# A recurrent-attention and token/channel-mixer kernel: batch 0's attention laid out by token slot, other filler matmuls, and a new instruction order

## The chip, the core and the metric

The kernel runs on one core of a Trainium2 chip. The core has a matrix engine (TensorE, PE in the profile; its weight loads are PEld), a vector engine (VectorE, DVE), an activation engine (ScalarE, ACT), a general engine (GpSimd, POOL) and a sync engine (SyncE, SP) that here only issues transfers. Each engine works through its own queue in program order; semaphores order work between engines. Matrix results land in PSUM, eight banks of 128 partitions by 512 float32; everything else lives in SBUF. The metric is the device time of one execution in microseconds, the median of several runs.

## The reference

```python
for t in range(S):                                   # attention: B, H, S, D = 4, 8, 768, 48
    state = alpha[:, :, t, :, None] * state + einsum('bhd,bhe->bhde', k[:, :, t], v[:, :, t])
    y[:, :, t] = einsum('bhd,bhde->bhe', q[:, :, t], state)
x = y.transpose(0, 2, 1, 3).reshape(4, 768, 384)
h = relu(x.transpose(0, 2, 1) @ w_tok1) @ w_tok2     # tokens: 768 -> 256 -> 768
u = x + h.transpose(0, 2, 1)
out = u + relu(u @ w_ch1) @ w_ch2                    # channels: 384 -> 1536 -> 384
```

Inputs and output are float32. Each of q, k, v and alpha is 4.7 MB, the weights are 6.3 MB and the output is 4.7 MB.

## The kernel before, in words

**Attention.** Each batch is cut into three tiles of 256 tokens; tile n (0 to 11) belongs to batch n // 3. A tile's tokens lie two to a partition: partition p holds tokens 2p (slot 0) and 2p+1 (slot 1). A chunk is 128 tokens, partitions 0 to 63 or 64 to 127, so a tile has two chunks (hf 0 and 1). For a tile the names in the program are: `ld_at`, `ld_kt`, `ld_qt`, `ld_vt` (loads of 393 KB each); `ln` or `ln1`/`lnP` (logarithm of alpha); `cum` or `cumw` (running sums of the logarithms by matmuls with a triangular matrix); `E` and `IE` (exp of the sums and of their negatives, on ACT); `kk` and `qq` (k times IE, q times E, in bf16); `vb` (v in bf16); `trk`, `trq` (PE transposes of kk and qq) and `evk`, `evq` (their copies out of PSUM); `G` (products of keys and queries per head, one per chunk), `mask` (causal mask, on DVE, also the copy out of PSUM); `K` (k times v, summed over a chunk), `s`, `sa`, `sm` (the recurrent state after a chunk); `ia`, `ib` (query times state), `y` (masked G times v, added to it in PSUM) and `x` (copy out, the mixer's input).

Tiles 0 to 2 are "wide": both slots go through `lnw`, `cumw`, `E`, `IE`. In tiles 3 to 11 slot 0's decay is folded in by products instead (`P`, `r1`, `k0a`, `q0r`). From tile 6 on the transposes are made by DMA (`dk`, `dq`, then `pq`).

In the kernel before, `G` by chunk puts slot 0's tokens of a chunk on partitions 0 to 63 and slot 1's on 64 to 127, so `y` can contract 128 tokens in one matmul of 128 rows. For that v has to be moved across partitions (`vs0`, `vs1`: `vswap`), and so have the keys for `K` (`ka`, `kb`, `kc`: `kturn`): copies of 64 partitions by 384 on ACT or POOL. `K` (`kfull`) is then four 128-row matmuls of 96 columns per chunk. The state is carried by `sa` (K plus old state, on DVE) and `sm` (times the decay, on DVE or POOL).

**Mixer.** For each batch: `t1` (12 matmuls of 384 columns, w_tok1), `ht` (relu), `t2` (12 matmuls, w_tok2), `u` (add, DVE), then u transposed: for batches 0 and 1 by PE (`up`, and `ut` copies it out), for 2 and 3 by DMA (`ux`); `c1` (24 groups of three matmuls, w_ch1), `rt` (relu, 24 on ACT or DVE), `c2` (24 groups of three, w_ch2), `o` (add, DVE) and `st` (store). Weights come in 16 loads of 393 KB (`ldw_`) and are cast to bf16 (`cw_`).

**Order.** The program is written under a manual schedule: the text ORDER lists every operation in the order of issue with the letter of its engine (t PE, s ACT, v DVE, g POOL, y SP), and BUFS gives each value its buffer. Dependencies between operations become semaphore waits. One more rule is in `shared`: operations that two engines run over a common SBUF port (the products, casts and shifts on DVE and POOL, those with `port=True`) are made to wait for the last such operation of the other engine, so the two never run them at once.

**Fillers.** `f1_...` and `f3_...` in ORDER are one or three matmuls of 512 columns of zeros into a bank that the next operation overwrites; nobody reads them. They stand before work of tiles 0 to 2 only.

The opening of ORDER before, up to the last `t1` of batch 0's first half:

```
ld_at1s ld_at0y ld_qt0y ld_vt0y ld_kt0s ld_at2y f1_cumw0t ln0s f3_cumw0t f1_trk1t f1_cumw1t f1_trk0t f3_cumw1t
f1_trq0t f3_trq0t ln1s ld_qt1y f1_trq1t cumw0t cumw1t E0s ld_at3y f3_trk1t IE0s Et0s qq0v vb0s ld_kt1y kk0v trq0t E1s
...
ldw_wt10s sa0_1v f1_y0t lnP3s qq2v IE2s Et2s ldw_wt11y cum3t ib0t IE3s r13s sm0_1v trq2t E3s evq2s G0_1t y1_0t sa1_1v
vb3g vs1_3s x1_0s G1_1t kk3v f1_y2t ldw_wt21y ld_qt3y mask1_1v kk2g ldw_wt20y f1_y1t mask0_1v vb2s ib1t y1_1t trk3t
vs0_2g vs1_2g trk2t evk3v ia1t ldw_wc13y f3_G02t f1_G02t sm1_1g evk2v kc2s ld_at5y P4g cw_wt10s x1_1v K2t ldw_wc14y
G0_2t sa0_2v cw_wt11s mask0_2v sm0_2g ka3s ln14s t1_0_0_0t ia2t G1_2t y0_1t t1_0_1_0t t1_0_1_1t y0_2t t1_0_0_1t vs0_3g
mask1_2v kc3s x0_1s ib2t kb3s lnP4s t1_0_1_2t ldw_wc15y q0r3v x0_2s y1_2t K3t t1_0_0_2t t1_0_1_3t ld_kt4y x1_2s qq3v
```

Of the kernel before, what the change touches and what calls it, by code (L numbers as in the profile page):

```python
# [96 lines left out]
NB = 3  # L97
NX = 6
# [12 lines left out]
WIDE = (0, 1, 2)  # L111

# [3 lines left out]
def build(g):  # L116
# [8 lines left out]
    def filler(nm, bank):  # L125
        return [P.op(f"f{z}_{nm}", {"PE": pe([512] * z)["PE"], "NONE": (0.0, 0.0)}, -100, writes=[bank],
                     emit=lambda e, z=z: g.fill(bank, z)) for z in (1, 3)]

    def attention(n):
# [8 lines left out]
        def fill(nm, bank):  # L138
            return filler(f"{nm}{n}", bank) if n < NB else []

        at, kt, qt, vt = V("in"), V("in"), V("in"), V("in")
        ld = {}
        for v, nm in ((at, "at"), (kt, "kt"), (qt, "qt"), (vt, "vt")):
            ld[nm] = P.op(f"ld_{nm}{n}", {"SP": (420.0, 420.0), "ACT": (374.0, 374.0)}, -90000.0 + 10 * n, writes=[v],
                          emit=lambda e, v=v, nm=nm: g.load(e, nm, v, b, k, ld[nm]), dma=("i", IN_NS, 1500.0, 650.0))
        la, E, IE = V("la"), V("E"), V("IE")
        pkk, pkq, vb = V("pkk"), V("pkq"), V("vb")
        k_in, q_in = [ld["kt"]], [ld["qt"]]
        if n in WIDE:
            lnp = O("ln", act(800, True), 0, writes=[la], reads=[at], preds=[ld["at"]], emit=lambda e: g.lnw(la, at))  # L150
            cb = V("pair")
            cum = O("cumw", pe([384] * 4 + [4] * 8 + [16]), 2, writes=[cb, E, IE], reads=[la], preds=[lnp] + fill("cumw", cb),
                    emit=lambda e: g.cumw(cb, la))
            e1 = O("E", act(768), 4, writes=[E], reads=[cb], preds=[cum], emit=lambda e: g.exps(E, cb, 1.0))
            et = O("Et", act(16), 6, writes=[E], reads=[cb], preds=[cum], emit=lambda e: g.exptot(E, cb))
            e2 = O("IE", act(768), 3, writes=[IE], reads=[cb], preds=[cum], emit=lambda e: g.exps(IE, cb, -1.0))
        else:
# [8 lines left out]
            e1 = et = O("E", act(400), 4, writes=[E], reads=[cb], preds=[cum], emit=lambda e: g.expE(E, cb))  # L166
            e2 = O("IE", act(384), 4, writes=[IE], reads=[cb], preds=[cum], emit=lambda e: g.expIE(IE, cb))
# [12 lines left out]
        if n < NX:  # L180
            bk, bq = V("one"), V("one")
            trk = O("trk", pe([128] * 8), 8, writes=[bk], reads=[pkk], preds=[kk] + fill("trk", bk),
                    emit=lambda e: g.trw(bk, pkk))
            evk = O("evk", either(dve(1024, True), act(1024)), 9, writes=[tpk], reads=[bk], preds=[trk],
                    emit=lambda e: g.trwev(e, tpk, bk))
            trq = O("trq", pe([128] * 8), 8, writes=[bq], reads=[pkq], preds=[qq] + fill("trq", bq),
                    emit=lambda e: g.trw(bq, pkq))
            evq = O("evq", either(dve(1024 * 1.065), act(1024 * 1.34)), 9, writes=[tpq], reads=[bq], preds=[trq],
                    emit=lambda e: g.qev(e, tpq, g.bank(bq).bitcast(BF16)))
        else:  # L190
            evk = O("dk", {"SP": (1240.0, 1240.0)}, 9, writes=[tpk], reads=[pkk], preds=[kk],
                    emit=lambda e: g.xbar(tpk, pkk), dma=("x", 1400.0, 1180.0, 480.0))
# [13 lines left out]
        nst = 2 if k < NB - 1 else 1
        kp = V("pair")
# [149 lines left out]
    for b in range(B):  # L357
        mixer(b)
# [91 lines left out]
class Emit:  # L450


    def __init__(self, tc, ctx, q, k, v, alpha, w, out):
# [61 lines left out]
        for t in self.T["pkq"] + self.T["pkk"]:  # L515
            dv.memset(t[:, :, :, D:64], 0.0)
# [358 lines left out]
```

## Time and profile before

| what | value |
|---|---|
| time, median of 3 runs (lowest to highest) | 167.82 us (167.51 to 168.41) |
| span of the profiled execution (its own time, first to last instruction) | 165.0 us |
| PE busy | 156.2 us, 95% |
| DVE, ACT, POOL busy | 121.2, 96.2, 68.7 us |
| transfers | 34.48 MB, 209 GB/s over the span |
| instructions | 4235 |

The span counts from the first instruction to the last; the run's time has in addition what lies before and after them, 2.8 us between the profiled span and the median. "Busy" of PE counts a matmul until its results are out, so back-to-back matmuls overlap, and it counts the fillers as well; only the spacing of matmuls says how fast the engine takes them. A row of the timeline gives start, length, engine, line, operation, operands and count, and in brackets how long the engine was idle before it and what ended that. A row of the chain gives start, length and what was running; "SPq" is the transfer queue of SP.

### The profile page before, as it was taken

What the parts mean: (1) busy time and instruction counts of PE and PEld (TensorE: products, weight loads), DVE (VectorE), ACT (ScalarE), POOL (GpSimd) and SP (SyncE); (2) the same over time, 40 slices, a digit from 0 to 9 for tenths busy, and PEclk for the clock granted to TensorE, in tenths of its full rate; (3) what the DMA queues carried; (4) which work ended last, traced back from release to release, by engine and by line L of the source; (5) the groups of instructions that cost most, each with busy time, mean ns of one, the idle gap of its engine ahead of it and who ended that gap; (6) DMA issues with size and microseconds to landing.
All of it is one profiled execution on the core that took longest, in us unless ns stands there. A gap on an engine that the chain in (4) does not pass through costs nothing.

```text
span 165.0 us, 4235 instructions
## 1 busy us (share of the span) xinstructions
PE 156.2 (95%) x1683; PEld 99.2 (60%) x1683; DVE 121.2 (73%) x210; ACT 96.2 (58%) x186; POOL 68.7 (42%) x84
## 2 busy tenths in 40 slices
PE   7969769999999999999999999999999999999992
PEld 2435446666666766576666666666666656656662
DVE  4098989989898898798878999989492455524422
ACT  3599987998877837939887746913614001514110
POOL 4025659497217475792388528973300000000000
PEclk9999999999999999999999999999999999999999
DMA  4999999999999999999989996898001136200213
GB/s 121 324 325 325 337 347 316 365 327 352 371 335 347 326 315 226 307 252 264 136 198 255 211 250 120 219 181 183 0 4 48 49 75 157 105 0 0 99 72 119
DMA packets 74531, 34.48 MB, mean 209 GB/s; under 512 B 67984, under 2 KB 73488, under 8 KB 74512
## 3 DMA queue, kind: packets, MB, share of 16 engines
q1 hardware_dynamic: 50576, 23.30, 55.2%
q10 hardware_dynamic: 23936, 10.91, 24.3%
q8 instruction: 13, 0.21, 0.5%
q14 instruction: 6, 0.05, 0.1%
HBM read 25.17 MB, written 4.72 MB: 181 GB/s over the span
## 4 chain that ended last, share of the span: by engine, by line
PE 83%; DMA 4%; SPq 3%; POOL 2%; issue 2%; ACT 2%; DVE 1%; POOLq 0%; DVEq 0%
PE ps L816 29%; PE ps L811 29%; PE ps L593 14%; PE ps L792 5%; DMA in<-in_v_dram 4%; PE ps L787 4%; SPq L534 3%; PE ps L654 1%; PE ps L803 1%; POOL pkk L642 1%; DVE gtm L700 1%; POOL vb L685 1%; ACT x L684 1%; POOL ss L753 1%; ACT E L626 0%
## 5 line engine op out<-in xcount | busy, mean ns | idle before, releaser
L816 PE MATMUL ps<-wc,rt 128*128 128x384 bf16 (+1 forms) x300 | 54.7, 320 | 0.0
L811 PE MATMUL ps<-ut,wc 128*128 128x384 bf16 x288 | 51.3, 326 | 0.0
L782 ACT ACTIVATE rt<-ps 128x384 bf16<-128x384 f32 x54 | 24.4, 490 | 35.4 <-PE ps L811 34.7
L811 PEld LDWEIGHTS <-wc 128*128 128x128 bf16 x288 | 27.1, 98 | 16.7
L816 PEld LDWEIGHTS <-rt 128*128 128x128 bf16 x300 | 27.5, 98 | 15.9
L700 DVE TENSOR_TENSOR gtm<-ps,mk 128x1024 bf16<-128x1024 f32 x24 | 28.7, 1219 | 4.8 <-PE ps L593 3.4
L784 DVE TENSOR_SCALAR rt<-ps 128x384 bf16<-128x384 f32 x42 | 21.7, 551 | 9.2 <-PE ps L811 9.2
L820 DVE TENSOR_TENSOR o<-ps,u 128x384 f32<-128x384 f32 (+1 forms) x25 | 13.1, 537 | 10.0 <-PE ps L816 9.1
L685 POOL CAST vb<-in 64x384 bf16<-64x384 f32 (+1 forms) x18 | 10.9, 608 | 15.2 <-DVE pkk L642 8.9
L593 PE MATMUL ps<-zs 128*128 128x512 bf16 x38 | 12.7, 452 | 2.9 <-DVE zs L496 1.1
L684 ACT CAST x<-ps 128x384 bf16<-128x384 f32 x17 | 7.8, 477 | 10.7 <-PE ps L593 10.5
L796 DVE TENSOR_TENSOR u<-ps,x 128x384 bf16<-128x384 f32 x24 | 11.8, 550 | 3.0 <-PE ps L792 3.0
L642 DVE TENSOR_TENSOR pkq<-in,E 128x768 bf16<-128x768 f32 x8 | 7.6, 954 | 5.4 <-ACT E L626 5.2
L787 PE MATMUL ps<-x,wt 128*128 128x384 bf16 x48 | 11.1, 325 | 0.5 <-DVE gtm L700 0.4
L684 ACT CAST vb<-in 64x384 bf16<-64x384 f32 (+1 forms) x18 | 11.1, 618 | 0.7 <-DMA in<-in_v_dram 0.2
L642 POOL TENSOR_TENSOR pkk<-in,IE 128x768 bf16<-128x768 f32 x5 | 9.1, 1816 | 4.9 <-DVE pkk L685 3.2
L753 POOL TENSOR_TENSOR ss<-tmp,E 128x384 bf16<-128x384 f32 x11 | 9.2, 833 | 3.2 <-DVE tmp L750 2.9
L750 DVE TENSOR_TENSOR tmp<-ps,ss 128x384 f32<-128x384 f32 x16 | 8.8, 552 | 1.0 <-PE ps L593 0.5
L792 PE MATMUL ps<-ht,wt 128*128 128x384 bf16 x48 | 9.5, 326 | 0.0
L593 PEld LDWEIGHTS <-gtm 128*128 128x128 bf16 x192 | 7.4, 96 | 2.7 <-DVE gtm L700 0.9
L593 PEld LDWEIGHTS <-tpk 48*64 48x64 bf16 x384 | 6.1, 106 | 4.9 <-issue 4.3
L593 PE MATMUL ps<-vb,gtm 128*128 128x48 bf16 x192 | 8.6, 183 | 0.4 <-DVE gtm L700 0.4
(91 smaller groups left out, 216.6 us busy)
## 6 DMA issues: line engine op xcount, KB each, us to landing
in<-in_moe_w_ch_dram SPq DMA_DIRECT2D x10, 384.0 KB, 6.2
in<-in_alpha_dram SPq DMA_DIRECT2D x9, 384.0 KB, 6.8
out_dram<-o SPq DMA_DIRECT2D x16, 192.0 KB, 2.5
in<-in_q_dram SPq DMA_DIRECT2D x7, 384.0 KB, 6.3
in<-in_v_dram ACTq DMA_DIRECT2D x7, 384.0 KB, 6.0
in<-in_k_dram ACTq DMA_DIRECT2D x6, 384.0 KB, 5.7
in<-in_k_dram SPq DMA_DIRECT2D x6, 384.0 KB, 6.2
in<-in_v_dram SPq DMA_DIRECT2D x5, 384.0 KB, 7.2
```

The lines of the kernel that those rows point to most:

```text
L593: return self.pe.matmul(out, lhsT=lhsT, rhs=rhs, start=start, stop=stop, skip_group_check=True)
L642: self.shared(self.eng[e].tensor_tensor(self.t(dst)[:, :, :, 0:D], self.t(src).rearrange("p h s d -> p s h d"), bass.AP(tensor=f.tensor, o ...
L684: return self.act.copy(d, s)
L685: return self.shared(self.eng[e].tensor_copy(d, s))
L700: self.nc.vector.tensor_tensor(self.t(gtm)[:, hf, :, :], self.pair(gp).rearrange("p a (j t) -> p (a j) t", t=128), bass.AP(tensor=m.tensor ...
L782: self.act.activation(d, s, AF.Relu)
L784: self.nc.vector.tensor_scalar_max(d, s, 0.0)
L787: self.pe.matmul(self.bank(bank)[:, 0:HD], lhsT=self.wt1[:, kc, m * 128 : m * 128 + 128], rhs=self.t(x), start=(kc == 0), stop=(kc == NS - 1))
L792: self.pe.matmul(self.bank(bank)[:, 0:HD], lhsT=self.wt2[:, kc, i * 128 : i * 128 + 128], rhs=self.t(hts[kc]), start=(kc == 0), stop=(kc = ...
L811: self.pe.matmul(self.bank(bank)[:, 0:HD], lhsT=self.wc1[:, kc, mc * 128 : mc * 128 + 128], rhs=self.t(ut)[:, 3 * half : 3 * half + 3, kc, ...
L816: self.pe.matmul(self.bank(bank)[:, 0 : cz - ca], lhsT=self.t(rts[mc][0])[:, i * 128 : i * 128 + 128], rhs=self.wc2[:, mc, ca:cz], start=( ...
L820: self.nc.vector.tensor_tensor(self.t(o)[:, ca:cz], self.bank(bank)[:, 0 : cz - ca], self.t(u)[:, i % 3, ca:cz], ALU.add)
```

## The change

1. **Batch 0 by token slot (tiles 0 to 2).** `G` is made by slot: for one slot's queries, both chunks of keys lie on the partitions where their tokens are, chunk 0 on 0 to 63, chunk 1 on 64 to 127 (`gslot`, `maskslot` with a second mask tile `mkw`). `y` and `K` then contract 64 rows at a time, the two chunks on the two halves of the array (`yslot`: 32 matmuls of 48 columns for the tile, `khalf`: 16 of 96 columns, 8 in the last tile). `vs0`, `vs1`, `ka`, `kb`, `kc` fall away in these tiles. The old state is added to K by a matmul with the identity (`A0`, `A1`: `kadd`, 384 columns), and `s` multiplies by the decay straight out of PSUM on DVE; `sa` and `sm` fall away in these tiles. Both chunks' y come from one operation, so both wait for both masks.
2. **E and the chunk totals in one.** `cumw` writes the totals' offset into both banks, and one `E` per tile covers what `E` and `Et` did.
3. **Fillers.** They may stand before more operations and come in counts of 1 to 12; every three of them become one float32 matmul, 64 columns of weights and 384 moving columns (`fill`). `zs`, their operand, moves into a buffer of `rt`.
4. **Loads.** Loads of tiles 0 to 5 and of the weights are issued by SP alone; before, nine of those forty were ACT's. The first three pieces of w_ch1 are cut by 256 columns over all rows instead of by 128 rows over 768 columns, so that `c1` of the first six column blocks needs one piece each.
5. **ORDER and BUFS are new throughout,** with other engines for many operations. `UP = (0, 1)`, u of batches 0 and 1 transposed by PE, stands the same in both kernels, and so do the tiles transposed by DMA (6 to 11).

```diff
+LOADQ = ({"SP": (420.0, 420.0)}, {"SP": (420.0, 420.0), "ACT": (400.0, 400.0)})
...
+        if wide:
+            kps = [V("one") for _ in range(nst)]
+            K = O("K", {"PE": (430.0, 560.0)}, 9.5, writes=kps, reads=[pkk, vb], preds=kk + [vc],
+                  emit=lambda e, first=before is None: g.khalf(kps, pkk, vb, first), mode="Y")
+            for hf in range(nst):
+                kp, s_, sp = kps[hf], V("ss"), states[-1]
+                KO = K
+                if sp is not None:
+                    KO = O(f"A{hf}_", pe([384]), 9.6 + hf, writes=[kp], reads=[sp[0]], preds=[K, sp[1]],
+                           emit=lambda e, kp=kp, s0=sp[0]: g.kadd(kp, s0))
+                so = O(f"s{hf}_", dve(384), 10 + hf, writes=[s_], reads=[kp, E], preds=[KO, et],
+                       emit=lambda e, s_=s_, kp=kp, hf=hf: g.sfirst(s_, kp, E, hf, wide))
+                states.append((s_, so))
...
+            yo = O("y", {"PE": (440.0, 580.0)}, 14, writes=yps, reads=[gtm, vb], preds=masks + [vc] + helds[0] + helds[1],
...
     def fill(self, bank, count):
-        for _ in range(count):
-            z = self.zs
-            z = bass.AP(tensor=z.tensor, offset=z.offset, ap=[list(z.ap[0]), [0, 4], [1, 128]])
-            self.mm(self.bank(bank), self.zs, z, True, True)
+        z, w = self.zs, self.zs.bitcast(F32)
+        for _ in range(count // 3):
+            m = bass.AP(tensor=w.tensor, offset=w.offset, ap=[list(w.ap[0]), [0, 6], [1, 64]])
+            self.mm(self.bank(bank)[0:64, 0:384], w, m, True, True)
+        for _ in range(count % 3):
+            m = bass.AP(tensor=z.tensor, offset=z.offset, ap=[list(z.ap[0]), [0, 4], [1, 128]])
+            self.mm(self.bank(bank), z, m, True, True)
...
+    def khalf(self, kps, pkk, vb, first):
+        kk, vv = self.t(pkk), self.t(vb)
+        for j in range(4):
+            for sl in range(2):
+                for hf, kp in enumerate(kps):
+                    ph = slice(hf * 64, hf * 64 + 64)
+                    self.mm(self.bank(kp)[:, 96 * j : 96 * j + 96], kk[ph, sl, 2 * j : 2 * j + 2, :],
+                            vv[ph, sl, 2 * j : 2 * j + 2, :], j == 0 and sl == 0, (first and hf == 0) and sl == 1)
+
+    def kadd(self, kp, s0):
+        self.mm(self.bank(kp)[:, 0:HD], self.idn, self.t(s0), False, True)
+
+    def yslot(self, yps, gtm, vb, first):
+        gg, vv = self.t(gtm), self.t(vb)
+        for h in range(H):
+            for sl in range(2):
+                for hf in range(2):
+                    ph = slice(hf * 64, hf * 64 + 64)
+                    self.mm(self.bank(yps[hf])[:, h * D : h * D + D], gg[ph, sl, 4 * (h % 2) + h // 2, :],
+                            vv[ph, sl, h, :], first[hf] and h == 0 and sl == 0, h == H - 1 and sl == 1)
```

The new ORDER from its start to batch 0's first `c2`, with the first two thirds of `c1` left out:

```
ld_at0y ln0s f8_cumw0t f1_cumw0t cumw0t IE0s E0s ld_kt0y ld_kt1y ld_qt0y kk0v qq0v f12_trq0t trq0t evq0v ld_at1y trk0t
ln1s cumw1t ld_vt0y IE1s evk0v ld_vt1y vb0g f2_G0_0t G0_0t kk1g G1_0t ld_qt1y K0t mask1_0v E1s s0_0v f4_A1_0t f1_A1_0t
A1_0t qq1g ld_at2y vb1s K1t ln2s s1_0v A0_1t ld_at3y ln13s r13s s0_1v cumw2t E2s P3g lnP3s mask0_0v trq1t evq1v trk1t
ld_qt2y qq2g evk1s A1_1t f8_G0_1t f2_G0_1t G0_1t G1_1t trq2t IE2s ib0t y0t ld_at4y ln14s ld_vt2y evq2s s1_1v vb2g P4g
mask0_1v cum3t E3s x1_0s ia1t mask1_1v f1_ib1t ib1t y1t ld_kt2y ld_kt3y kk2v k0a3v IE3s K2t A0_2t kk3v ka3g x0_1s
x1_1s trk2t evk2v f2_trk3t trk3t s0_2v G0_2t ldw_wt10y ld_vt3y ld_qt3y G1_2t x0_0s ia2t kc3s cw_wt10s f1_t1_0_1_0t
t1_0_1_0t t1_0_1_1t mask0_2v ib2t t1_0_1_2t t1_0_0_0t t1_0_0_1t vb3g t1_0_0_2t kb3s mask1_2v y2t ldw_wt11y vs0_3s
x1_2v vs1_3s lnP4s K3t cw_wt11s cum4t x0_2v t1_0_0_3t t1_0_0_4t q0r3g t1_0_0_5t t1_0_1_3t t1_0_1_4t t1_0_1_5t s0_3v
sa1_3v ldw_wt20y cw_wt20s ht_0_0s qq3g trq3t ldw_wt21y ldw_wc13y cw_wt21v cw_wc13g ht_0_1s t2_0_3t evk3v u_0_3v
t2_0_2t u_0_2v t2_0_0t u_0_0v t2_0_1t E4s IE4s u_0_1v t2_0_5t u_0_5v evq3s ldw_wc15y up_0_1t t2_0_4t ut_0_1s sm1_3g
cw_wc15g ldw_wc14y cw_wc14g ld_kt4y up_0_0t ut_0_0s G0_3t u_0_4v G1_3t up_0_2t mask1_3v c1_0_8_0t ut_0_2s k0a4g r14s
...
ia4t t1_1_1_0t rt_0_11_0s y0_4t t1_1_1_1t cw_wc22s qq5g vs1_4g
K4t c1_0_10_1t rt_0_10_1s t1_1_0_0t t1_1_0_1t x0_4s mask1_4v cw_wc20g sa0_4v trq5t ldw_wc21y cw_wc21g evq5s c2_0_1_0t
```

408 lines of the change are left out of this document (220 added, 188 removed), and 22 rows, old and new, of the table BUFS.

## The prediction

> **What bounds the kernel now.** First view: the page's first part and a table of busy time by stretch. Columns of the table: stretch, its length, busy time and count on PE, PEld, DVE, ACT, POOL, then granted clock, transfer share and GB/s.
>
> ```profile
> PE 156.2 (95%) x1683; PEld 99.2 (60%) x1683; DVE 121.2 (73%) x210; ACT 96.2 (58%) x186; POOL 68.7 (42%) x84
> 0.00:7.60 7.60, 6.55 (x29) 2.74 (x30) 2.00 (x18) 2.86 (x3) 2.00 (x12) 1.00 0.79 214
> 7.60:31.40 23.80, 19.20 (x314) 12.41 (x311) 21.00 (x27) 21.64 (x38) 12.88 (x17) 1.00 1.12 334
> 31.40:37.30 5.90, 5.90 (x90) 4.25 (x90) 5.29 (x11) 5.51 (x10) 5.62 (x7) 1.00 1.10 338
> 37.30:51.70 14.40, 14.40 (x138) 9.38 (x136) 13.09 (x23) 12.29 (x27) 6.59 (x8) 1.00 1.11 351
> 72.90:162.00 89.10, 88.99 (x870) 56.18 (x868) 60.76 (x104) 40.16 (x84) 27.45 (x28) 1.00 0.57 126
> 162.00:165.00 3.00, 0.00 (x0) 0.00 (x0) 0.36 (x1) 0.00 (x0) 0.00 (x0) 1.00 0.45 159
> ```
>
> From 31.4 on PE never waits. The tail of 3.0 is the last add and store. So the time is the moment at which PE becomes full, plus the work left by then, plus the tail. Second view, the chain of waits, for what sets that moment:
>
> ```profile
> 14.06 7.23 DMA in<-in_v_dram
> ...
> 23.31 1.83 POOL pkk L642
> ...
> 25.20 0.50 POOL vb L685
> ...
> 26.34 0.84 POOL ss L753
> 27.20 0.56 DVE tmp L750
> 27.76 1.14 DVE gtm L700
> 28.90 0.49 ACT pkk L684
> ...
> 32.26 0.27 PE ps L593 x6
> 32.53 0.46 PE ps L654 x8
> 32.99 2.06 PE ps L792 x12
> 35.05 0.17 PE ps L593 x4
> ...
> 37.51 2.48 PE ps L811 x15
> ...
> 62.22 0.57 PE ps L593 x32
> ```
>
> Tile 2's loads end at 21.3; then come kk2 on POOL, shifts of v (L685), sm, sa, a mask and a shift of keys on ACT before x is there. cum4 (0.27) and trq3 (0.46) fill PE until t2, ib3 (0.17) follows it. t2 runs from 33.0 and c1 from 37.5, at 165 ns a matmul (2.48/15), which is the steady rate.
>
> **The change part by part.** Third view, prices: groups by line and shape (mean ns behind the busy time), and rows of the timeline.
>
> ```profile
> L700 DVE TENSOR_TENSOR gtm<-ps,mk 128x1024 bf16<-128x1024 f32 x24 | 28.7, 1219 | 4.8 <-PE ps L593 3.4 <-ACT lf L590 1.0
> L642 POOL TENSOR_TENSOR pkk<-in,IE 128x768 bf16<-128x768 f32 x5 | 9.1, 1816 | 4.9 <-DVE pkk L685 3.2 <-DVE pkk L642 1.1 <-POOL in L634 0.5
> L642 DVE TENSOR_TENSOR pkk<-in,IE 128x768 bf16<-128x768 f32 x7 | 6.7, 954 | 1.1 <-POOL vb L685 0.6 <-issue 0.3
> L684 ACT COPY kt<-pkk 64x384 bf16<-64x384 bf16 x13 | 6.6, 508 | 3.5 <-PE ps L593 2.7 <-POOL pkk L642 0.6
> L685 DVE COPY tpq<-ps 128x1024 bf16<-128x1024 bf16 x3 | 3.9, 1306 | 0.6 <-PE ps L654 0.6
> L685 DVE COPY tpk<-ps 128x1024 bf16<-128x1024 bf16 x4 | 2.6, 683 | 0.0
> L747 DVE TENSOR_TENSOR ss<-ps,E 128x384 bf16<-128x384 f32 x4 | 2.2, 548 | 0.0
> L626 ACT ACTIVATE E<-ps 128x768 f32<-128x768 f32 x3 | 2.4, 808 | 1.1 <-PE ps L593 1.1
> L684 ACT CAST wt<-in 128x768 bf16<-128x768 f32 x3 | 2.4, 834 | 0.0
> 5.00:10.00 5.00, 4.64 (x45) 2.48 (x44) 1.48 (x2) 3.90 (x7) 0.00 (x0) 1.00 1.17 325
> 1.05 5.73 PE L593 MATMUL ps<-zs 128*128 128x512 bf16 x15 [1.05 <-DVE zs L496]
> 5.00 1.58 ACT L587 ACTIVATE la<-in 128x768 bf16<-128x768 f32 x2 [2.92 <-DMA in<-in_alpha_dram]
> 8.52 0.96 DVE L642 TENSOR_TENSOR pkq<-in,E 128x768 bf16<-128x768 f32 x1 [5.19 <-ACT E L626]
> 10.00 0.81 PE L593 MATMUL ps<-zs 128*128 128x512 bf16 x3
> ```
>
> *Token slots.* Gone from tiles 0 to 2: thirteen shifts (six vs, two ka, two kb, three kc), 13 x 0.5 = 6.5 us of ACT and POOL; four sa (0.55, DVE) and four sm. New on DVE: four s at 0.55, so DVE gains only about 0.6, the one sm it had. New on PE: four matmuls of 384 columns, 4 x 0.165 = 0.7. K and y have twice the matmuls. Whether 64-row pairs run side by side the trace doesn't show; the nearest row is G, 32 matmuls of 128 columns in 0.57, where one after the other would take 32 x 55 ns = 1.8: its quarter tiles do overlap. Bounds: nothing when they pair, and when they don't about +0.3 for each of K0, K1 and +0.4 for each y (40 and 23 ns a matmul, by width), 1.9 in all. I take the pairing. Either way it lies between 7.6 and 31.4, where PE is idle for 4.6 and runs fillers besides; only K2 and y2 are on the path, 0.4 at worst.
>
> *E with the totals* drops three small activations, priced at nothing. *Loads:* the number of bytes is unchanged. Before, two alpha loads are under way together and both are there at 5.0, when ln0 and ln1 run back to back. Alone, alpha 0 lands between 3.8 (one load, 1.2 us at 325 GB/s, less) and 5.0; I take 4.0. Load n of the new order lands at 5.0 + 1.21(n-2): 393 KB at 325 GB/s.
>
> *Fillers.* 42 units of 512 columns replace 38, nearly all where PE waits. The price of the float32 form isn't in the trace. Bounds: one pass of 384 columns, 0.165, and the three matmuls of 512 that it replaces, 0.65 warm. I take 0.65. The Trainium skill, page "FP8 and Floating Point Precision", TensorE Precision Notes, says true float32 goes four times through the array; by that my estimate is 4 x 384 = 1536 columns, the same 0.65, and no run here shows it.
>
> *The walk.* I follow the new ORDER engine by engine with these prices, each step at the latest of its inputs and of its engine (0.04 for a hand-over, as from E's end to qq0 at 8.52).
> Tile 0: ln0 4.0 to 4.84; the first fillers end at 4.9, still at half rate; cumw0 to 6.2; IE0 7.05, E0 7.75; kk0 8.05, qq0 8.9 (kt0, load 2, and qt0, load 4, are there at 5.0 and 7.4); trq0 9.55, evq0 10.85, evk0 11.45; ln1 waits for load 5, 8.6, and ends at 9.6, cumw1 10.65, IE1 11.5, E1 12.2; G0, G1 12.15; mask1 13.4, s0 13.85, A1 14.2, s1 14.8.
> Tile 1: kk1, qq1 on POOL 11.55 to 15.2; A0 15.15, s0 15.75; mask0 of tile 0 16.9; evq1 on DVE 18.1, evk1 on ACT 18.2. PE runs 10 units of filler from 17.0 to 19.1 ahead of G0_1: 0.85 late, counted in. G's to 19.7, trq2 20.1; masks 20.75 and 21.85.
> Tile 2: qq2 on POOL 18.7 (load 11 and E2); kk2 is on DVE now, 21.8 to 22.7 (load 14, 19.5, isn't the last input); k0a3, kk3 24.05; evk2 24.65, s0 25.1, mask0 26.35, mask1 27.45, y2 27.95, both x 29.0.
> Mixer 0: w_tok1's halves are loads 16 and 19, cast by 26.1 and 28.7; the last t1 at 30.1; ht, both on ACT, 30.05 and 30.65; w_tok2, loads 20 and 21, cast by 30.4; t2 from 30.7, against 32.99. Then six u on DVE after evk3, 31.2 to 34.1; up_0_2 waits for the last of them; c1 from 34.7, against 37.51; w_ch1's second half, loads 22 to 24 (31.6), is cast by 32.6.
>
> *The sum.* c1 starts 37.5 - 34.7 = 2.8 sooner. By then the kernel before has also done cum5 and ib3, which the new one has not: 0.27 and 0.17 of PE. That leaves 2.8 - 0.45 = 2.35. Some 25 hand-overs lie on the walk; those that I set at 0.04 measure 0.03 to 0.1, for which I take off 0.35. Gain 2.0. From 34.7 on I find PE full again: in c1 of batch 0 the closest steps are w_ch1's first pieces (loads 27 to 29, 35.3 to 37.7, one block each as it is needed), w_ch2's (loads 34 to 36, cast just as c2 begins near 50.7) and the shared port, where P5 and five casts on POOL wait for kk4 on DVE, and q0r4 behind them until 41; each has up to 1 us to spare. Then 165.0 - 2.0 = 163.0 of span. The median of the runs is 2.8 above the profiled span; with that, **165.8**. The tail stays: the last add and half store stand as before, with one more 196 KB store just ahead of them on ACT's queue, 0 to 0.6 us at 325 GB/s, and I take 0.
>
> The change also names u of batch 1 by TensorE. UP is (0, 1) on both sides; that part costs and brings nothing.
>
> **The rivals.** *ACT holds PE up in c1 of batch 0 (slower).* Between the first c1 and the first c2 the new ORDER gives ACT 32 operations, 19 of them relus, 17.0 us at their rows' means; before it was 25 and 13.4. PE has 24 x 0.49 for c1 and 4.6 of attention and t1 there, 16.3. Against it: evq5, 1.3 of the 17.0, comes after PE's last matmul of that stretch. For it: in the same stretch before, ACT was busy for 12.29 of 14.40, 85%. At 85% its 17.0 would take 19.9, 3.6 longer than PE's work, and nothing later gives that back, since PE is full: 169.4. The gain is used up once ACT falls under 17.0/18.3 = 93%, and slower by over 0.5% is reached at 89%.
>
> *The opening is no shorter (same).* If alpha 0 lands only at 5.0, everything up to cumw1 moves by up to 1.0; with 0.08 a hand-over instead of 0.05 another 0.7 goes: 167.5. For it: transfers are saturated from 3 us on either way, and the 21st load ends w_tok2 near the same time in both orders. Against it: from 12 us on my walk waits for DVE's queue and not for a load.
>
> *The clock falls (slower).* The first 15 fillers took 5.73 us and three of them at 10.0 took 0.81: PE starts at half rate and speeds up after some 4.5 us, although the clock column says 1.00 throughout. If float32 fillers do not hold the full rate, the walk's PE steps up to t2, some 7 us of streaming, double for about half of their time: 3.5 longer, 169.3. Against it: before, PE had 4.6 us of idle in 23.8 and stayed fast. The Trainium skill, "TensorE: Matmul & The Clock Gate", Part 1, says that a window of about 3.4 us of idle halves the clock; the longest hole in my walk is about 1 us, so by that rule this rival fails, but no run here shows whether these fillers count as work.
>
> **How the numbers follow.** Forecast case 0.61, opening no shorter 0.14, ACT 0.17, clock 0.08. About 0.5% (0.84 us, 166.98 to 168.66) is what a measurement of this kernel can tell from no change. So faster 0.61, same 0.14, slower 0.25. The forecast case's own range is 164.2 (DVE's waits in the walk sum to 3.1, half of them gone) to 166.9 (alpha 0 at 5.0). The whole range goes up to the ACT rival's 169.4 and leaves out the rest of that and the gains beyond: 164.2 to 169.4.
>
> **What would show it.** ln0 near 4.0 and E0's end near 7.8; no L685 or L684 copy of 64 partitions before tile 3's; the second x of tile 2 near 29, t2 from about 31, c1 from about 35; then PE over 98% busy with matmuls at 165 ns. Wrong would be: holes of PE in c1 or c2 of batch 0 that end on an rt of ACT or on a weight cast; zeros' matmuls far from 0.65 each, or matmuls at double length after 6 us; K or y of tiles 0 to 2 longer than 0.4; and, beyond my walk, PE waits of batch 1 or later, each of which would be paid in full.

## The result, and the profile after

The changed kernel takes 166.21 us (median of 20 runs), the kernel before on the same chip 167.41 us (20 runs): a ratio of 0.9945, 95% interval 0.9921 to 0.9969. It is faster, by about half a per cent. A second series (e11 below) gives 0.9934, 0.9909 to 0.9959. The profiled span fell from 165.0 to 164.2. Of the 64 executions of the kernel before that ran beside the experiments, 29 show a mean granted clock of 0.99 or less and a median of 167.49, the other 35 one of 166.64, while all 32 of the changed kernel (this series and e11) are at 0.997 or more with a median of 166.09, so that at the full clock the gain is 0.55 in the medians and 0.8 in the profiles.

The first line below is from the page's first part, the others from a table of busy time by stretch (the same stretches, and the same columns, as those shown of the kernel before; the last row runs from the start of `c1` to PE's last matmul).

```profile
PE 158.2 (96%) x1753; PEld 99.2 (60%) x1753; DVE 117.8 (72%) x207; ACT 93.6 (57%) x174; POOL 72.4 (44%) x84
...
7.60:31.40 23.80, 22.73 (x401) 13.94 (x400) 19.14 (x25) 17.58 (x30) 13.13 (x11) 1.00 1.09 319
...
37.30:51.70 14.40, 14.40 (x171) 9.76 (x169) 12.80 (x19) 12.09 (x28) 9.50 (x11) 1.00 1.02 311
...
35.72:161.27 125.55, 124.72 (x1267) 80.02 (x1264) 91.42 (x151) 68.77 (x136) 53.58 (x57) 1.00 0.73 189
```

In the opening (7.6 to 31.4) DVE lost 1.9 us of work and ACT 4.1, and PE is busy for 22.73 of the 23.80 instead of 19.20, with fillers. In `c1` of batch 0 PE is full. The same last row for the kernel before:

```profile
37.34:162.00 124.66, 124.55 (x1257) 79.74 (x1254) 92.54 (x156) 66.12 (x137) 48.14 (x49) 1.00 0.73 180
```

These two rows and the tail behind them are the whole account. Before: `c1` starts at 37.34, PE has 124.55 of work left and 0.11 of idle, and 3.0 remain for the last add and store: 165.0. After: 35.72 + 124.72 + 0.83 of idle + 2.9 = 164.2. So the change starts `c1` 1.62 sooner, leaves 0.17 more work behind that point, and pays 0.72 in new idle time.

The way to `c1`, from the timeline (start, length, engine, line, operation, tiles; in brackets the idle time ahead and what ended it):

```profile
4.27 0.84 ACT L641 ACTIVATE la<-in 128x768 bf16<-128x768 f32 x1 [2.18 <-DMA in<-in_alpha_dram]
...
8.17 0.95 DVE L704 TENSOR_TENSOR pkq<-in,E 128x768 bf16<-128x768 f32 x1
...
9.11 0.84 ACT L641 ACTIVATE la<-in 128x768 bf16<-128x768 f32 x1 [1.12 <-DMA in<-in_alpha_dram]
...
10.09 0.65 PE L647 MATMUL ps<-la,u 128*128 128x384 bf16 x3
...
12.34 0.51 PE L647 MATMUL ps<-vb,pkk 64*128 64x96 bf16 x16
...
17.13 0.33 PE L647 MATMUL ps<-ss,idn 128*128 128x384 bf16 x1
17.39 2.47 PE L647 MATMUL ps<-rt 128*64 128x384 f32 x8
19.79 0.64 PE L647 MATMUL ps<-tpq,tpk 48*64 48x128 bf16 x32
...
21.09 0.57 PE L647 MATMUL ps<-vb,gtm 64*128 64x48 bf16 x32
...
22.53 0.95 DVE L704 TENSOR_TENSOR pkk<-in,IE 128x768 bf16<-128x768 f32 x1
...
23.54 0.51 PE L647 MATMUL ps<-vb,pkk 64*128 64x96 bf16 x8
23.98 0.34 PE L647 MATMUL ps<-ss,idn 128*128 128x384 bf16 x1
...
29.21 1.02 DVE L747 CAST x<-ps 128x384 bf16<-128x384 f32 x2 [0.71 <-ACT la L638]
...
31.54 1.98 PE L875 MATMUL ps<-ht,wt 128*128 128x384 bf16 x10
```

These are `ln0`, `qq0`, `ln1`, `cumw1`, `K0`, `A1_1`, the fillers ahead of `G0_1`, `G` of tile 1, `y0`, `kk2`, `K2` and `A0_2`, both `x` of tile 2, and `t2`.

Nearly all of the new idle time is one hole, near 121 (0.78 of the 0.83). The timeline there, one fence of ACT, PE and SP's queue:

```profile
115.97 2.13 SPq L726 DMA_TRANSPOSE tpk<-pkk  x1
...
120.38 0.51 ACT L746 COPY pkk<-pkk 64x384 bf16<-64x384 bf16 x1 [2.60 <-POOL vb L747]
...
121.40 0.51 ACT L746 COPY kt<-pkk 64x384 bf16<-64x384 bf16 x1
...
121.97 0.34 PE L647 MATMUL ps<-vb,kt 128*128 128x96 bf16 x4 [0.78 <-ACT kt L746]
```

PE's `K10` waits for `kb10` (ACT, 121.40). In ACT's queue `kb10` stands behind `kc11` (120.38), a copy for the next tile, for which ACT idles 2.60. `kc11` overwrites keys that the DMA transpose `dk11` (issued from 115.97) still reads. The page names a copy of v on POOL as what ended `kc11`'s wait; in e11 below, the same kernel once more, it names the transpose (2.42 at 120.15), and so it does in e1.

### The profile page after: what moved, and what is told of

The parts are those of the page before. It is cut to its first block, busy times and chain, and to the rows that moved or that the text cites. A ratio compares the mean times of both kernels' runs of the same rounds, so it can differ in the third digit from the quotient of the medians.

```text
span 164.2 us, 4340 instructions
## 1 busy us (share of the span) xinstructions
PE 158.2 (96%) x1753; PEld 99.2 (60%) x1753; DVE 117.8 (72%) x207; ACT 93.6 (57%) x174; POOL 72.4 (44%) x84
## 4 chain that ended last, share of the span: by engine, by line
PE 83%; DVE 6%; ACT 4%; issue 3%; DMA 2%; POOL 1%; POOLq 0%
PE ps L899 27%; PE ps L894 26%; PE ps L647 18%; PE ps L870 4%; PE ps L875 4%; PE ps L716 2%; DMA ut<-u 2%; PE ps L886 1%; DVE u L879 1%; DVE vb L747 1%; DVE tpk L747 1%; ACT kt L746 1%; ACT vb L746 1%; DVE pkk L704 1%; DVE gtm L762 1%
## 5 line engine op out<-in xcount | busy, mean ns | idle before, releaser
L762 DVE TENSOR_TENSOR gtm<-ps,mk 128x1024 bf16<-128x1024 f32 x18 | 21.5, 1218 | 2.0 <-PE ps L647 2.0
L747 POOL CAST vb<-in 128x768 bf16<-128x768 f32 (+1 forms) x14 | 9.6, 687 | 15.7 <-DMA in<-in_v_dram 8.5
L647 PE MATMUL ps<-rt 128*64 128x384 f32 (+1 forms) x33 | 12.8, 510 | 1.1 <-DVE rt L539 1.1
L632 POOL TENSOR_TENSOR in<-in 128x384 f32<-128x384 f32 x9 | 9.0, 1000 | 10.9 <-DVE wc L747 3.9
L704 POOL TENSOR_TENSOR pkq<-in,E 128x768 bf16<-128x768 f32 x7 | 12.7, 1818 | 1.5 <-DMA in<-in_q_dram 1.1
L746 ACT CAST x<-ps 128x384 bf16<-128x384 f32 x12 | 5.6, 484 | 8.7 <-PE ps L647 8.6
L704 DVE TENSOR_TENSOR pkk<-in,IE 128x768 bf16<-128x768 f32 x7 | 6.7, 953 | 3.4 <-ACT IE L691 3.2
L778 DVE TENSOR_TENSOR gtm<-ps,mkw 128x1024 bf16<-128x1024 f32 x6 | 7.2, 1220 | 2.1 <-PE ps L647 2.1
L700 POOL TENSOR_TENSOR in<-in,lf 128x384 f32<-128x384 f32 x7 | 7.0, 999 | 3.7 <-ACT rt L865 2.5
L647 PE MATMUL ps<-vb,gtm 128*128 128x48 bf16 (+1 forms) x240 | 8.4, 182 | 0.0
```

Source lines behind the costliest of these rows:

```text
L647: return self.pe.matmul(out, lhsT=lhsT, rhs=rhs, start=start, stop=stop, skip_group_check=True)
L704: self.shared(self.eng[e].tensor_tensor(self.t(dst)[:, :, h0:h1, 0:D], self.t(src)[:, h0:h1].rearrange("p h s d -> p s h d"), bass.AP(tens ...
L747: return self.shared(self.eng[e].tensor_copy(d, s))
L762: self.nc.vector.tensor_tensor(self.t(gtm)[:, hf, :, :], self.pair(gp).rearrange("p a (j t) -> p (a j) t", t=128), bass.AP(tensor=m.tensor ...
```

## The experiments

My theory after this: the gain comes from the opening alone. The lone first load gives the lead, the fillers let PE use it, the slot layout keeps ACT and POOL from losing it, and a hole of 0.8 gives part of it back. The rivals: the slot layout alone is the gain; the first load alone is; the fillers do nothing; the hole is of one execution and not of the order. A ratio is to the kernel before, run beside it on the same chip.

**e1: the hole's cause.** `kc11` behind `kb10` and behind the two copies of v for its own tile.

```diff
 ORDER
-... c2_2_0_2t kc11s st_1_5y ... vs1_11s vs0_11s K10t
+... c2_2_0_2t st_1_5y ... vs1_11s vs0_11s kc11s K10t
```

> The changed kernel with one operation moved in ORDER: kc11 (ACT) goes behind kb10, vs1_11 and vs0_11. Theory: the only hole of PE after c1 begins (0.78 us at 121.2) is K10 waiting for kb10, which stands on ACT behind kc11, and kc11 waits for the DMA transpose that still reads its tile. With kc11 behind, the hole is gone and the span falls from 164.2 to about 163.4; ratio to before about 0.990. Rival: the hole comes from something else (POOL's shift of v, which the trace names) and only moves; span 164.0 to 164.3, ratio 0.994.

Measured: 165.45 us, ratio 0.9897, 0.9858 to 0.9935. A table from `c1`'s start, then `kb10` and `kc11` at its new place on ACT:

```profile
35.97:161.00 125.03, 124.86 (x1267) 80.01 (x1264) 91.38 (x151) 68.61 (x136) 54.28 (x58) 1.00 0.74 191
...
118.77 0.51 ACT L746 COPY kt<-pkk 64x384 bf16<-64x384 bf16 x1
...
120.80 0.51 ACT L746 COPY pkk<-pkk 64x384 bf16<-64x384 bf16 x1 [0.34 <-DMA tpk<-pkk]
```

PE's idle time after `c1`'s start is 0.17 (125.03 less 124.86) instead of 0.83, and the releaser of `kc11` is now the transpose itself, as thought. The transpose is over only at 120.80 here; `kb10`, no longer behind that wait, runs at 118.77. So the hole belongs to the place of one copy in ACT's queue. In this execution `c1` started 0.25 later than in the changed kernel, since `cumw0` still met PE at half its rate (three matmuls of 384 columns in 1.16 at 5.07, against 0.86 at 5.16), which is why the span, 164.0, shows less of it.

**e2: the form of the fillers.** The changed order with each float32 filler as three bfloat16 matmuls of 512 columns, as before.

```diff
-        for _ in range(count // 3):
-            m = bass.AP(tensor=w.tensor, offset=w.offset, ap=[list(w.ap[0]), [0, 6], [1, 64]])
-            self.mm(self.bank(bank)[0:64, 0:384], w, m, True, True)
-        for _ in range(count % 3):
+        for _ in range(count):
```

> The changed kernel with every float32 filler matmul put back as three bf16 matmuls of 512 columns. Theory: one float32 filler takes as long as the three, so cumw0, t2 and c1 stand within 0.2 us of the changed kernel and the ratio to before stays at 0.994 to 0.995. Rival: the float32 form is what keeps the opening on time (it is shorter, or holds the clock better); then c1 starts 0.5 us or more later and the ratio is 0.998 or above.

Measured: 165.14 us, 0.9876, 0.9839 to 0.9913. Its timeline:

```profile
5.13 0.65 PE L647 MATMUL ps<-la,u 128*128 128x384 bf16 x3
...
17.05 2.32 PE L647 MATMUL ps<-rt 128*128 128x512 bf16 x10
19.60 0.64 PE L647 MATMUL ps<-tpq,tpk 48*64 48x128 bf16 x32 [0.23 <-ACT tpk L743]
...
35.53 1.79 PE L891 MATMUL ps<-ut,wc 128*128 128x384 bf16 x10
```

Faster than both of my expectations: the float32 form is no gain, and all four runs (165.03 to 165.30) are shorter than any of the changed kernel's 32 (165.38 and up). Ahead of `G0_1` (17.05) ten matmuls stream in 2.15 and `G0_1` then waits for `evk1`; in the changed kernel two float32 and four bfloat16 matmuls took from 17.39 to 19.79, 2.40. The weight loads show why (changed kernel, PEld):

```profile
17.76 0.14 PEld L647 LDWEIGHTS ps<-rt 128*64 128x64 f32 x1 [0.19 <-issue]
18.08 0.14 PEld L647 LDWEIGHTS ps<-rt 128*64 128x64 f32 x1 [0.18 <-issue]
18.82 0.55 PEld L647 LDWEIGHTS <-rt 128*128 128x128 bf16 x4 [0.60 <-issue]
```

A float32 matmul runs as two records, 0.32 apart (17.76, 18.08): 0.64 each, my 0.65. But the first bfloat16 weights after them come 0.74 later, not 0.32. Four records at 0.32 and four matmuls at 0.215 make 2.15; the rest of the 2.40, 0.25, comes with the change of form. It doesn't reach `c1` here, since `G0_1` waits for `evk1`: `c1` is 0.19 sooner (35.53), and 0.24 of lead stands already at `trq0` (8.94 against 9.18), because `cumw0` meets PE at the full rate (0.65 at 5.13). It does so in all three kernels of this order with bfloat16 fillers (e2, e8, e10) and in two of the six with float32 ones (e9, and e4, where it starts only at 5.85); whether the form or chance decides that is open. The hole at 121 isn't there in this execution; 0.45 of idle stands at 100 to 105 instead, so it depends on the timing ahead of it as well as on `kc11`'s place.

**e3: no fillers.** All `f` operations are left out of ORDER; nobody reads their results.

> The changed kernel with no fillers at all. If the fillers keep the matrix engine at its full rate, cumw0 and every matmul of the opening run at half rate here (512 columns would be 0.43, 384 columns 0.32), c1 starts 1 to 3 us later than at 35.7, and the span is 165.5 to 167. If they do nothing for the rate, the opening is the same or a few tenths sooner, span 163.8 to 164.3.

Measured: 167.33 us, 1.0008, 0.9975 to 1.0042. The timeline of PE:

```profile
17.24 1.17 PE L646 MATMUL ps<-la,u 128*128 128x384 bf16 x3
...
18.82 0.61 PE L715 MATMUL ps<-idn,pkq 128*128 128x128 bf16 x8
...
37.14 1.14 PE L893 MATMUL ps<-ut,wc 128*128 128x384 bf16 x6
```

Three matmuls of 384 still take 1.17 instead of 0.65 in tile 2 (17.24); from 18.82 PE is at the full rate (eight transposes in 0.61, as in the changed kernel). `c1` starts 1.42 later than in the changed kernel, and the whole gain is gone. So the fillers are worth as much as the change, by bringing PE to its full rate before the walk and not by the form of them. The granted-clock column reads 1.00 in these stretches, so the rate has to be read from the matmuls.

**e4: the first load shared.** The changed kernel with the second alpha load first on ACT's queue, under way together with the first.

```diff
 ORDER
-ld_at0y ln0s f8_cumw0t ... evq0v ld_at1y trk0t
+ld_at1s ld_at0y ln0s f8_cumw0t ... evq0v trk0t
```

> The changed kernel with the load of alpha of tile 1 issued first on ACT's queue, so that it shares the first microseconds with alpha of tile 0, as in the kernel before. Rival to the token slots: if the earlier first load is what the change gains from, ln0 starts 0.7 us later (5.0 instead of 4.27), the whole opening moves, c1 starts at 36.4 and the span is 164.9, ratio 0.999. Theory: from 12 us on the opening is bound by the queues of DVE, ACT and POOL and by tile 1 and 2's loads, and alpha 1 is there sooner; c1 moves by 0 to 0.4, span 164.2 to 164.6.

Measured: 166.98 us, 1.0013, 0.9983 to 1.0042. ACT, then DVE, then PE:

```profile
4.96 0.84 ACT L641 ACTIVATE la<-in 128x768 bf16<-128x768 f32 x1 [2.88 <-DMA in<-in_alpha_dram]
...
7.78 0.96 DVE L704 TENSOR_TENSOR pkk<-in,IE 128x768 bf16<-128x768 f32 x1 [3.69 <-ACT IE L691]
9.22 0.96 DVE L704 TENSOR_TENSOR pkq<-in,E 128x768 bf16<-128x768 f32 x1 [0.48 <-ACT la L641]
...
36.78 1.46 PE L894 MATMUL ps<-ut,wc 128*128 128x384 bf16 x8
```

I was wrong here. `ln0` is 0.69 later, `kk0` 0.48 (7.78 against 7.30), `qq0` 1.05 (9.22 against 8.17), and the 1.05 goes through unchanged to `c1` (1.06). `qq0` doesn't need the `ln1` that the page names; `qt0` is now the fifth load instead of the fourth, and the fifth load of the changed kernel lands at 9.11 (`ln1` there). So about half of the 1.05 is the shared load of alpha and the rest the later place of q. I had held that DVE's queue paces the walk from 12 on and would take up a late load. It doesn't: DVE idles 4.66 of the 23.80 between 7.6 and 31.4, each time for PE or ACT, so the walk is one chain of hand-overs without slack, and a delay at its head moves all of it.

**e5: the slots alone.** The kernel before, its loads, fillers and order, with the slot layout: `vs`, `ka`, `kb`, `kc` and `Et` of tiles 0 to 2 left out, `sa` as a matmul (`A`), `sm` as `s` on DVE, `y0` and `y1` one operation.

```diff
 ORDER
-... vs0_0 vs1_0 ka0 kb0 kc0 ... sa0_1v ... sm0_1v ... y0_1t ... y1_1t
+... A0_1t s0_1v ... y1t
```

> The kernel before, its ORDER, loads, fillers and w_ch1 pieces kept, with only the token slots of tiles 0 to 2 (and E with the totals in one): the thirteen shifts left out, A and s in the place of sa and sm, one y per tile at the place of the later of the two. If the slots are what shortens the opening, c1 starts 0.7 to 1.5 us before 37.3 and the ratio is 0.991 to 0.996. After the shared first load took the whole gain away, the rival: the slots are hidden behind the queues of DVE and ACT, c1 starts between 36.9 and 37.5 and the ratio is 0.997 to 1.003.

Measured: 171.8 us, 1.0277, 1.0223 to 1.0331. PE's timeline, then a table by microsecond:

```profile
30.35 0.33 PE L642 MATMUL ps<-ss,tpq 128*128 128x96 bf16 x4 [1.62 <-DVE gtm L770]
...
31.59 1.14 PE L862 MATMUL ps<-x,wt 128*128 128x384 bf16 x3
...
31.00:32.00 1.00, 1.00 (x38) 0.77 (x35) 0.21 (x1) 0.31 (x1) 0.00 (x0) 0.60 1.05 419
32.00:33.00 1.00, 1.00 (x8) 0.58 (x6) 1.00 (x2) 0.95 (x3) 0.00 (x0) 0.50 1.06 338
...
34.00:35.00 1.00, 1.00 (x26) 0.87 (x21) 1.00 (x2) 0.65 (x2) 0.00 (x0) 0.69 1.17 361
```

In the old order the layout loses. `y` of a tile now needs both masks, and PE's queue, laid out for the old halves, stands behind DVE, once for 1.62. `c1` starts at 41.08, 3.74 later than before. Part of that is the clock: here the granted clock does fall, to 0.60, 0.50, 0.50 and 0.69 from 31 to 35, which costs 1.7 of PE's time just when `t1` streams (three matmuls in 1.14). The profiled execution is the shortest of the six, and in the others the mean granted clock goes down to 0.97, so in them the clock takes more than 1.7; without it `c1` would be some 2.0 later (3.74 less 1.7, an estimate). So the layout needs the new order; it isn't a gain by itself.

**e7: the first load alone.** The kernel before with `ld_at0` first and alone, key and query of tile 0 behind it, and `ln1`, `vb0`, `cumw1`, `E1` and four filler operations (six matmuls) moved behind tile 0's own steps.

```diff
 ORDER
-ld_at1s ld_at0y ld_qt0y ld_vt0y ld_kt0s ld_at2y
+ld_at0y ld_kt0y ld_qt0y ld_at1y ld_vt0y ld_at2y
```

> The kernel before with only the first loads changed: alpha, k, q of tile 0 and then alpha of tile 1, v of tile 0, all on SP; ln1, vb0, cumw1 and E1 stand behind tile 0's first steps, and six filler units move from ahead of cumw0 to behind it. If the gain is that of the lone first load, ln0 starts near 4.25, the opening moves by 0.7 to 1.0, c1 starts at 36.3 to 36.7 and the ratio is 0.994 to 0.996. If this order of the old layout cannot use it (tile 1 comes later, and ACT's queue sets the pace), c1 stays within 0.4 of 37.3, ratio 0.998 to 1.004.

Measured: 166.9 us, 1.0009, 0.9974 to 1.0044. ACT and PE:

```profile
4.15 0.84 ACT L587 ACTIVATE la<-in 128x768 bf16<-128x768 f32 x1 [2.06 <-DMA in<-in_alpha_dram]
...
10.57 0.81 ACT L626 ACTIVATE E<-ps 128x768 f32<-128x768 f32 x1 [0.73 <-PE ps L593]
11.40 0.51 ACT L684 COPY kt<-pkk 64x384 bf16<-64x384 bf16 x1
11.82 1.00 ACT L684 COPY tpk<-ps 128x1024 bf16<-128x1024 bf16 x1
...
12.87 0.38 PE L593 MATMUL ps<-zs 128*128 128x512 bf16 x1 [2.11 <-ACT tpk L684]
...
37.24 0.98 PE L811 MATMUL ps<-ut,wc 128*128 128x384 bf16 x5
```

`ln0` is 0.85 sooner than before, but `evk0`, the copy that `G0` waits for, comes at 11.82, after 11.29 before: on ACT it stands behind `E1` of tile 1 (10.57), which itself waits for PE, and behind a shift of keys (11.40), and PE idles 2.11 for it. `c1` starts at 37.24, 0.1 sooner. The lead is lost in ACT's queue; how much by the shifts and how much by the place of `E1` this run doesn't part.

**e9: the shifts' time put back.** The changed kernel with thirteen unread copies of 64x384, six on ACT and seven on POOL, where the layout before has its shifts.

```diff
+    def again(self, e, v):
+        m = self.mk[0:64]
+        m = bass.AP(tensor=m.tensor, offset=m.offset, ap=[list(m.ap[0]), [0, 3], [1, 128]])
+        self.copy(e, self.t(v).bitcast(BF16)[64:128, 0:HD].rearrange("p (a c) -> p a c", a=3), m)
 ORDER
-... vb2g P4g
+... vb2g z0_2g z1_2g P4g
```

> The changed kernel with the thirteen shifts' time put back where the layout before has them: thirteen copies of 64x384 on ACT (six) and POOL (seven) in tiles 0 to 2, of a constant into a scratch tile that nobody reads. They are extra work: no other step waits for their data. If the layout keeps the lead of the first load because it takes 6.5 us off ACT and POOL, c1 starts 0.5 to 2 us later than in the changed kernel (35.7), and the time is at that of the kernel before or above it. If only the waits that the shifts put between a load and K or y mattered, and not the engines' time, c1 moves by under 0.3 us and the ratio stays near 0.994.

Measured: 166.77 us, 0.9986, 0.9952 to 1.0019. POOL, DVE and PE:

```profile
20.91 1.07 POOL L757 COPY tmp<-mk 64x384 bf16<-64x384 bf16 x2
22.06 1.01 POOL L637 TENSOR_TENSOR in<-in 128x384 f32<-128x384 f32 x1
...
23.11 0.96 DVE L709 TENSOR_TENSOR pkk<-in,IE 128x768 bf16<-128x768 f32 x1 [0.73 <-POOL in L637]
...
36.31 1.95 PE L904 MATMUL ps<-ut,wc 128*128 128x384 bf16 x11
```

`c1` starts 0.59 later than in the changed kernel, and `kk2` on DVE already 0.58 (23.11 against 22.53): the two copies on POOL hold up `P4`, and by the shared-port rule `kk2` waits for `P4`. The steps of tile 1 up to 20 aren't later than in the changed kernel (`G0_1` at 19.55 against 19.79), so the copies up to there cost nothing. So the missing shifts are worth 0.6 in the new order, 0.8 counted from `G0_1`, through POOL and the port; the ratio's interval still touches that of the changed kernel run beside it.

**e6: fewer fillers ahead of `G0_1`.** e1's edit, with `f8_G0_1` made `f6_G0_1` and `lnP3` behind `IE2`.

```diff
 ORDER
-E2s P3g lnP3s mask0_0v ... f8_G0_1t f2_G0_1t G0_1t G1_1t trq2t IE2s
+E2s P3g mask0_0v ... f6_G0_1t f2_G0_1t G0_1t G1_1t trq2t IE2s lnP3s
```

> The changed kernel with kc11 moved as before, and in tile 1: lnP3 (ACT) behind evk1 and IE2, and eight filler units ahead of G0_1 cut to six. Theory: G0_1 waits until IE2 has read the PSUM banks that it writes (IE2 ends at 19.41, G0_1 begins at 19.79), so 0.5 less on ACT ahead of IE2 starts both masks of tile 1 0.5 to 0.7 sooner and, DVE being full from there to tile 2's masks, c1 as well: 35.3 instead of 36.0; ratio 0.986. Rival: tile 2's loads or ACT take the place, c1 moves by less than 0.2, ratio 0.989 to 0.990.

Measured: 165.76 us, 0.9915, 0.988 to 0.995. PE's timeline:

```profile
17.41 0.33 PE L647 MATMUL ps<-ss,idn 128*128 128x384 bf16 x1
...
19.64 0.64 PE L647 MATMUL ps<-tpq,tpk 48*64 48x128 bf16 x32
...
106.31 4.87 PE L894 MATMUL ps<-ut,wc 128*128 128x384 bf16 x29 [1.35 <-DMA ut<-u]
```

From `A1_1`'s start to `G0_1`'s it is 2.23 here. In the changed kernel it is 2.66 (17.13 to 19.79), and 2.66 again in e1, e9 and e11, although the page names another releaser of `G0_1` from run to run (`IE2`, the copy `evk1`, an `lf`). So it is the fillers in front that set `G0_1`, and the two fewer (0.43) are what moved `c1` from e1's 35.97 to 35.57; whether `lnP3`'s move adds anything is open. The gain was given back at once: a hole of 1.35 at 105, where `c1` of batch 2 waits for the DMA transpose of `u`, `ux_2_0`, which stands behind `dq10` in SP's queue.

**e8 and e10: the edits together.** e8 is e6 with bfloat16 fillers and `ux_2_0` ahead of `dq10`; e10 is the changed kernel with bfloat16 fillers, e1's `kc11` and the same `ux_2_0`.

```diff
 ORDER
-... rt_2_1_1s dq10y ux_2_0y k0a10g
+... rt_2_1_1s ux_2_0y dq10y k0a10g
```

> Both moves of the last kernel, bf16 fillers for the float32 ones, and the DMA transpose of u of batch 2's first half ahead of that of tile 10's queries on SP's queue, since c1 of batch 2 waited 0.45 us for it with the bf16 fillers. Sum of the single results: c1 at 35.0 to 35.3, no hole of PE after it, span near 162.7, ratio 0.982 to 0.985. If the moves overlap, the ratio is that of the bf16 fillers alone, 0.9876.

> The changed kernel with three edits: fillers of three bfloat16 matmuls of 512 columns in place of one float32 matmul, kc11 on ACT behind vs0_11, and ux_2_0's DMA transpose ahead of dq10 on SP's queue. By my account of the hole at 121 (0.8) and of the one at 105 to 110, PE has no hole over 0.3 after c1 starts, c1 starts at 35.5 to 35.8, the span is 163.2 to 163.6 and the ratio about 0.986. If waits only move to the next tight place, the span stays at 163.5 to 164.0 and the ratio at 0.988 to 0.990.

Measured: e8 165.34 us, 0.9885, 0.9843 to 0.9927; e10 165.14 us, 0.9877, 0.9842 to 0.9913. In e8 loads ran at 295 GB/s from 5 to 10 and at 271 from 10 to 14 (324 and 322 in the changed kernel), `cumw1` came at 11.34 instead of 10.09, and `c1` at 36.04 instead of the 35.0 to 35.3 that I expected; from there PE idles at most 0.46 (124.50 busy of 124.96). e10's `c1` and its one hole over 0.3:

```profile
35.59 2.60 PE L891 MATMUL ps<-ut,wc 128*128 128x384 bf16 x15
...
103.85 0.64 PE L647 MATMUL ps<-tpq,tpk 48*64 48x128 bf16 x32 [0.33 <-ACT tpq L743]
```

e10's span is 163.4, inside my first expectation, and its ratio is nearer to the second: the hole at 121 is gone, and one of 0.33 stands at the next tight place. It beats both kernels, by 1.2% against the change's 0.6%, and its longest run (165.31) is under the shortest of the changed kernel beside it (165.38); e1 and e2 alone measure about as much, and the intervals don't tell the three apart.

**e11: the changed kernel again**, beside e9 and e10.

> The changed kernel as it is, for comparison on the same chip: ratio 0.992 to 0.997, c1 at 35.5 to 35.9, and the hole of PE near 121 again if it belongs to the order and not to one execution.

Measured: 165.88 us, 0.9934, 0.9909 to 0.9959, span 164.0, `c1` at 35.63, and 0.60 of idle between 120 and 125. The hole is of the order; e4 has it too (0.58), e2 and e9 have none at that place.

**What the runs part and what not.** Taken out one at a time, the fillers are worth 1.42 at `c1`, the lone first load with q's place 1.06 and the shifts' time 0.59, where the whole change gained 1.62 there. They don't add up: each needs the others. `E` with the totals, the loads on SP alone, the pieces of w_ch1 and the order by itself were not tried apart.

## Why the prediction was right, and where it was not

The verdict came out, and the time (165.8 against 166.21, ratio 0.9945) came out in part by luck. The span, which my sum is about, did not as well: 163.0 predicted, 164.2 measured, a gain of 0.8 instead of 2.0. The 2.8 that I added is not what lies outside the span: each of the 64 executions of the kernel before that ran beside the experiments is 1.7 longer than its own span (1.66 to 1.77), and the 2.8 set the span of one execution against the median of three longer ones. With 1.7 I would have said 164.7, 1.5 too low.

The 1.2 that the span missed is made up so: `c1` came 1.62 sooner where I had 2.8 (0.17 of it because the chain's 37.51 is 37.34 in PE's timeline), 1.18 short; new idle time 0.72; against these the 0.35 that I had set aside for hand-overs, 0.28 of work left and 0.07 of tail.

- **Time = the moment PE is full + work left + tail.** Right: both accounts above close to within 0.1.
- **First load and `ln0`.** 4.0 predicted, 4.27 measured; `qq0` ends at 9.12 (8.9). Right mechanism, 0.27 and 0.22 short. The fifth load is in at 9.11, where my rule of 5.0 + 1.21 a load gave 8.6; 4.27 + 4 x 1.21 gives it, so the spacing was right and the start of the row was not.
- **"From 12 us on my walk waits for DVE's queue and not for a load."** Wrong, by e4: a load later at the head goes through one to one. The rival of an opening no shorter was thereby cheaper to fall into than I priced it: I gave it 167.5, and e4 is at no change.
- **Shifts gone, 6.5 us of ACT and POOL.** Right that they stood in the way, but their worth in the new order is 0.6 to 0.8 (e9), on POOL; and the layout alone is a loss of 2.8% (e5), part of it by the clock, which no step of mine said.
- **64-row pairs side by side.** Right for `K`: 16 matmuls take 0.45 from `K0`'s start to the next instruction (12.34 to 12.79), and `K2` with eight unpaired 0.44 (23.54 to 23.98). `y` takes 0.50 (21.09 to 21.59) where, by my 23 ns a matmul, pairing would give 0.37 and one after the other 0.74: only in part side by side. Both are over the 0.4 that I had named as a sign of being wrong; for `K` that bound was too low, since eight alone take 0.44, for `y` the sign holds. (My 1.9 for no pairing is 1.8 by its own terms.)
- **Float32 filler 0.65.** Right: 0.64. The Trainium skill, "FP8 and Floating Point Precision", TensorE Precision Notes, has true float32 go four times through the array. The trace agrees: four times the 0.165 of 384 columns is 0.66. What I left out is the 0.25 that comes with going back to bfloat16. With it the fillers ahead of `G0_1` take 2.40, 0.3 more than my ten units did.
- **The walk, `c1` at 34.7.** The term that failed most: 35.72. Against my times the slip is 0.22 at `qq0`, 0.69 at `G0_1` (19.79 against 19.1: late start and the fillers), 0.78 at `kk2`'s end, 1.2 at the end of both `x` (30.23), 0.84 at `t2` and 1.02 at `c1`. I had set 0.35 aside for hand-overs; the chain has no slack, so each of them counted.
- **Work left.** I took off 0.45 for `cum5` and `ib3`; the rows differ by only 0.17, so the rest of the work is 0.28 shorter. The ten matmuls of these two (1267 against 1257) are the only difference in number: all other kinds are as many in both, and the 0.28 lies in how they follow each other. Where was not traced.
- **"From 34.7 on I find PE full again."** Right in `c1` of batch 0: 14.40 of 14.40, and 16.55 of 16.55 up to the first `c2`. Wrong later: 0.83 of idle, near 121. I had named PE waits of batch 1 or later as something beyond my walk that would be paid in full; they were.
- **ACT holds PE up (0.17).** Fell. I counted 17.0 of ACT work between the first `c1` and the first `c2`; over those 16.55 us ACT is busy for 13.88, 84%, in 31 records. The 32nd operation that I counted, `evq5` (1.3), runs behind the first `c2`, as I had said; the other 1.8 is that neighbours overlap at their ends (two relus in a row take 0.87, not twice 0.49), and means add that time twice. A busy share of 84% was no sign of a bound.
- **The clock (0.08).** Fell for this kernel: `cumw1` at 10.09 runs at the full rate, so float32 fillers count as work. But e3 shows that the opening without fillers fails on it, and e5 that the old order with the new layout does. Over all runs the mean granted clock is 0.996 or more in each of the 83 executions with the new order and its fillers, and 0.99 or less in five of ten without them (e3), in five of twelve of e7 and in all six of e5. The Trainium skill, "TensorE: Matmul & The Clock Gate", Part 1, has the clock fall to a half after an idle window of some 3.4 us and rise again after a busy one as long. e5's stretch agrees in length: at a half, 0.80 + 1 + 1 + 0.62 of the four microseconds make 3.4. It doesn't in the cause: the longest idle of PE ahead of it is 1.62, in three microseconds in which PE was busy for 1.38.

## What to carry to other kernels

When an opening is a chain of hand-overs, ask where each engine's idle time in it ends: if always on another engine, a later load at its head costs its full delay at the end, however idle the engines look. Price a layout only together with the order that it runs in, since here the layout alone lost 2.8% (part of it by the clock), the first load alone gained nothing, and the two with the new order and its fillers gained 0.6%. And once PE is full, look for copies made early for a later tile that stand in a queue ahead of work for this one: moving one such copy of 0.5 took away nearly all of the 0.8 of idle time. Last, set the time of an execution against its own span: the span of one and the median of others differed by 2.8 here, the time and the span of the same execution by 1.7.

## What the runs showed of the hardware

- A float32 matmul of 64 output rows by 384 columns is two records 0.32 apart, 0.64 in all. The first bfloat16 weights after it come 0.74 after its last weights, and two such matmuls with four of bfloat16 behind them take 2.40, 0.25 more than their spacings add up to.
- PE ran at half its rate up to tile 2 with no fillers (three matmuls of 384 columns in 1.17 at 17.24), with the granted-clock column at 1.00, while in e5 the same column fell to 0.50 in mid-kernel, 3.4 us at a half by its four values, after an idle time of 1.62 at most.
- 16 matmuls of 64 rows by 96 columns on two row halves take 0.45, and eight on one half 0.44.
- With one alpha load under way it is in at 4.27, with two at 4.96, and after that loads come every 1.2 us on one queue (325 GB/s).
